# One burst of twelve score tiles for two pairs of heads, in the attention of rounds two to four of a float32 attention and gated-MLP kernel

## The chip, the cores and the metric

The kernel runs on one core of a Trainium2 chip. The metric is device time in microseconds (us). Before the change it is 634.46 us, the median of three runs (633.99 to 634.55).

## The reference, cut to what matters

```python
scores = scale * np.matmul(q, k.transpose(0, 1, 3, 2)) - np.log(S)   # scale = 1/8
attn = 1.0 / (1.0 + np.exp(-scores))                                  # a sigmoid, no softmax
x = np.matmul(attn, v)            # 8 batches, 12 heads, S = 448, 64 wide; then [8, 448, 768]
h = np.maximum(x @ w_in, 0.0)     # w_in [768, 1024]
u, v = h[..., :512], h[..., 512:]
v_n = (v - mean(v)) / np.sqrt(var(v) + 1e-06)
v_s = np.einsum('ts,bsd->btd', w_spatial, v_n) + b_spatial[None, :, None]
return ((u * v_s) @ w_out).astype(np.float32)
```

All in float32. The change touches only the first three lines' part of the program.

## The kernel before, in words

**Rounds.** Two batches make a round, so there are four (`m` = 0 to 3, called rounds one to four here). A round does the attention of its two batches, then the MLP (`v_half`, `spatial`, `u_half`, `outputs`). Round one has an attention of its own (`first_attention`); `attention(m)` (L1107) does rounds two to four. It is a generator: `outputs` of the round before runs its first two pieces (`splits(0)` and `splits(1)`) at its two `between()` calls, L982 and L994, and the main loop the rest (L1345).

**Units and pairs.** A unit is one load of two heads' q and k (tile `raw`, four buffers). Two neighbouring units share one load of v (tile `v`, three buffers) and make a pair; a round has six pairs, p = 0 to 5, units 2p and 2p + 1. A unit's q and k are cut into a high float32r part and a rest (`attention_splits`, L291, into a tile `qks` of three buffers): a copy (L116) and a subtraction (L117), which stand on VectorE except for the first units of a round.

**A pair** (`pair`, L1164). Six score tiles: for each, `attention_scores` (L309) issues three matmul steps for two heads side by side (64 rows each, L339) into a PSUM tile of two banks, and ScalarE applies the sigmoid (L347) from there to an SBUF tile `at`. Then the splits for the next pair are issued (L1177). Then six product tiles (`attention_values`, L353): `at` times v, two heads side by side (64 columns each, float32, L373), added up in one more PSUM tile, `pav`. `copy_sums` (L1148, with the copy in L1150) has VectorE copy `pav` to a tile `whole`. TensorE's records show a product matmul as two.

**PSUM.** `banks` (L128) hands out four tiles in turn, the one longest not handed out first. Scores and `pav` alike take them: seven a pair.

**SBUF.** Ten tags (`big`, `tmp`) hold the `at` tiles and the `whole` tiles, handed out from the list `free`. Every finished pair keeps one for its `whole`.

**The rest of keys.** 448 keys are three tiles of 128 and a rest of 64. The rests of all pairs are done after pair 4 in two groups of three, p = 0, 3, 1 and then 4, 2, 5 (`short_scores`, L1138, and `short_values`): their operands come by loads of their own, tile `last`, two DMAs each (`last_loads`, L1125; 64 KB and 448 KB). Pair 5 comes after them.

**Order of queues.** Each engine's instructions run in the order in which they are emitted (`in_program_order`, L19). So does SyncE (SP), which issues all these DMAs and waits where a buffer isn't free yet. After pair p the loop at L1200 issues the next loads of q and k (L1203) or `last` (L1206), a load of v (L1212), which waits until pair p's products have read the buffer, some weight work (`load_weights`; in round two this is GpSimd's `u_sums` and `v_sums`, with stores to HBM), and in rounds three and four a load of factors (`block_load`, L1195).

Of the kernel before, what the change touches and what calls it, by code (L numbers as in the profile page):

```python
# [9 lines left out]
F32 = mybir.dt.float32  # L10
F32R = mybir.dt.float32r
U32 = mybir.dt.uint32
AF = mybir.ActivationFunctionType
ALU = mybir.AluOpType

P = 128
# [20 lines left out]
def attn_gmlp_kernel(  # L37
# [25 lines left out]
    nc = tc.nc  # L63
    B, NHP, _, _ = qk.shape
    S = out.shape[3]
    D = P // 2
    NCC = out.shape[1]
    DM = NCC * P
    F = w_in.shape[1] // (4 * NCC)
# [9 lines left out]
    QK = 1.0 / math.sqrt(D)  # L79
# [43 lines left out]
    def slot(tags, name, shape=(P, 2, 512), dtype=F32):  # L123
        tag = tags.pop(0)
        tags.append(tag)
        return work.tile(list(shape), dtype, tag=tag, name=name, bufs=1)
# [134 lines left out]
    def load_weights(n):  # L261
        for _ in range(n):
            next(weights[0], None)
# [24 lines left out]

    parts_of = {}

    def attention_splits(b, hp):  # L291
        raw = loaded[b, hp][:, HALF:]
        s = work.tile([P, 2, 2 * S], F32R, tag="split", name=f"qks_{b}_{hp}", bufs=3)
        if b == 0 and hp < 2:

            for cols, copy in ((slice(REST, PART), nc.vector.tensor_copy), (slice(0, FULL - P), nc.scalar.copy)):
                split(s[:, 0, cols], s[:, 1, cols], raw[:, cols], nc.vector.tensor_copy if hp else copy)
        else:
            scalar = b == 1 or b == 0 and hp not in (1, 2) or b % 2 == 0 and b and hp < 2
            split(s[:, 0, :PART], s[:, 1, :PART], raw[:, :PART], nc.scalar.copy if scalar else nc.vector.tensor_copy)  # L300
        parts_of[b, hp] = s
# [7 lines left out]
    def attention_scores(b, hp, t, tag=None, slots=big, raws=None):  # L309

        psc = banks(f"psc_{b}_{hp}_{t}", tag)
        heads = [slice(j * D, (j + 1) * D) for j in range(2)]
        if t == NFULL:
            for odd in range(2):
                if raws is None:
                    raw = loaded[b, hp + odd]
                    key, query = raw[:, :HALF], raw[:, HALF + REST :]
                else:
                    key, query = raws[:, odd, :HALF], raws[:, odd, HALF:]
                for j, rows in enumerate(heads):  # L320
                    nc.tensor.matmul(  # L321
                        psc[odd * HALF : (odd + 1) * HALF, j, :S],
                        key[rows],
                        query[rows],
                        start=True,
                        stop=True,
                    )
        elif b == hp == 0 and t % (NFULL + 1) == 0:
            raw = loaded[b, t // (NFULL + 1)][:, HALF:]
            for j, rows in enumerate(heads):  # L330
                nc.tensor.matmul(  # L331
                    psc[:, j, :S], raw[rows, FULL - P : FULL], raw[rows, REST:PART], start=True, stop=True
                )
        else:
            s = parts_of[b, hp + t // (NFULL + 1)]
            k = (t % (NFULL + 1) + NFULL - 1) % NFULL * P
            for i, (a, e) in enumerate(FIRST_TERMS if b == hp == 0 else TERMS):
                for j, rows in enumerate(heads):
                    nc.tensor.matmul(  # L339
                        psc[:, j, :S],  # L340
                        s[rows, a, k : k + P],
                        s[rows, e, REST:PART],
                        start=i == 0,
                        stop=i == len(TERMS) - 1,
                    )
        at = slot(slots, f"at_{b}_{hp}_{t}")[:, :, :S] if isinstance(slots, list) else slots
        nc.scalar.activation(at, psc[:, :, :S], AF.Sigmoid, bias=bias_s, scale=QK)  # L347
        return at
# [4 lines left out]
    def attention_values(b, hp, t, at, last_v=None, tag=None):  # L353

        key = b, hp, last_v is None
        if key not in pav_of:
            pav_of[key] = banks(f"pav_{b}_{hp}_{t}", tag)
        pav = pav_of[key]
        total = NFULL + 1 if b < 2 else NFULL if last_v is None else 1
        for odd in range(2):  # L360
            if t == NFULL:
                rows = slice(odd * HALF, (odd + 1) * HALF)
            elif (t > NFULL) == odd:
                rows = slice(0, P)
            else:
                continue
            unit = key, odd
            count[unit] = count.get(unit, 0) + 1
            start, stop = count[unit] == 1, count[unit] == total
            vt = values[b, hp][:, t] if last_v is None else last_v  # L370
            for j in range(2):
                heads = slice(j * D, (j + 1) * D)
                nc.tensor.matmul(pav[heads, odd, :S], vt[rows, heads], at[rows, j], start=start, stop=stop)  # L373
        return pav[:, :, :S]

    def x_parts(b, hp):
# [206 lines left out]

    xs = {}

    others = [const.tile([P, 2, F // 2], F32R, name=f"other_{i}") for i in range(2)]
    other_places = [t.rearrange("p a f -> p (a f)")[:, 16 : 16 + S] for t in others]

    v_second, x_rest = {}, {}

# [516 lines left out]
    def attention(m):  # L1107

        first = 2 * NHP * m
        free = []  # L1110
        shorts, wholes, lasts, held = {}, {}, {}, {}
        copy = nc.vector.tensor_copy

        def unit(p):
            return units[first + 2 * p]

        def loads(*ns):
            for n in ns:
                attention_loads(*units[first + n])

        def splits(*ns):
            for n in ns:
                attention_splits(*units[first + n])

        def last_loads(p):  # L1125
            b, hp = unit(p)
# [21 lines left out]
        def copy_sums(p, pav, copy):  # L1148
            whole = slot(free, f"whole_{m}_{p}")[:, :, :S]
            copy(whole, pav)  # L1150
            wholes[p] = free.pop(), whole
# [12 lines left out]
        def pair(p):  # L1164
            full, tags = [], []
            for t in (*FIRST, *SECOND):
                if p == NHP - 1 and t == TILES - 1:
                    place = work.tile([P, 2, S], F32, tag="v", name=f"at_last_{m}", bufs=3)
                    full.append((*unit(p), t, attention_scores(*unit(p), t, None, place)))
                else:  # L1170
                    full.append((*unit(p), t, attention_scores(*unit(p), t, None, free)))
                    tags.append(free.pop())
            if p < 2:
                load_weights(1)
            nc.scalar.copy(mark, full[-1][-1][:1, 0, :1])
            if p + 1 < NHP:
                splits(2 * p + 2, 2 * p + 3)  # L1177
            for args in full:
                pav = attention_values(*args)
            free.extend(tags)  # L1180
            if p + 1 < NHP:
                copy_sums(p, pav, copy)
            return pav

        splits(0)
        yield
        splits(1)
        yield
        free.extend((*big, *tmp))
        if m == 1:  # L1190
# [4 lines left out]
        def block_load(k):  # L1195
            nc.sync.dma_start(v_block(m, k).bitcast(F32), w_v_dram[:, k])

        loads(4, 5)
        value_loads(*unit(2))
        for p in range(NHP - 1):  # L1200
            pair(p)
            if p < 3:
                loads(2 * p + 6, 2 * p + 7)  # L1203
            else:
                for u in ((0, 3), (1, 4, 2, 5))[p - 3]:
                    last_loads(u)  # L1206
            if p == 2:
                last_v = work.tile([P, 2 * NFULL + 1, P], F32, tag="v", name=f"last_v_{m}", bufs=3)
                lasts_of = v[2 * m : 2 * m + 2, :, :, NFULL].rearrange("b g p c -> p b g c")
                for i, b, gs in ((0, 0, slice(0, 2)), (2, 0, slice(2, 3)), (3, 1, slice(0, 3))):  # L1210
                    nc.sync.dma_start(last_v[:, i : i + gs.stop - gs.start], lasts_of[:, b, gs])
            elif p < 4:  # L1212
                value_loads(*unit(p + 3 - p // 3))
            load_weights((1, 1, 2, 3, 8)[p])
            if m > 1 and p < 4:
                block_load(p)
            elif m == 1 and p == 4:
                for k in range(4):
                    block_load(k)
        first_ones, others_of = (0, 3, 1), (4, 2, 5)  # L1220
        for p in first_ones:
            short_scores(p)
# [44 lines left out]
        xs.update({(S2, c): unit_of(raws[c]) for c in range(NH)})  # L1267
        xs[S1, 0] = unit_of(raws[3])
        xs[S4, 0], xs[S3, 0], xs[S1, 1], xs[S4, 1], xs[S4, 2], xs[S3, 2] = free
        xs[S1, 2] = tuple(other_places)  # L1270
        xs[S3, 1] = tuple(part[:, :S] for part in parts)
        for c in range(NH):
            xs[A11, c], xs[A12, c] = (halves(x_s[:, :, 2 * c + i, :S]) for i in range(2))
# [161 lines left out]
```

## Time and profile before

| | |
|---|---|
| median of three runs | 634.46 us |
| the profiled execution | 635.16 us |
| its span, first to last instruction | 633.4 us |
| TensorE busy | 99% |
| VectorE, ScalarE, GpSimd busy | 70%, 54%, 17% |
| granted TensorE clock, mean | 1.000 |
| score matmuls (L339), product matmuls (L373) | 93.5 and 116.9 us busy |

Busy time of TensorE adds what pipelined matmuls overlap, so it says that the engine is never without work, not how fast it goes. How fast it goes is read from the number of matmuls that start in a stretch. A row of the timeline merges instructions of one kind that follow each other; its time goes from the first start to the last end. In a DMA row the time is that of the issue; the transfer lands later.

### The profile page before, as it was taken

How to read it: one execution, taken by the hardware profiler on the slowest of the kernel's cores; microseconds unless marked ns; L12 is line 12 of the kernel's file. 1: busy time of each engine (PE TensorE's matmuls, PEld its weight loads, DVE VectorE, ACT ScalarE, POOL GpSimd, SP SyncE). 2: the span in 40 equal slices, each digit the busy share in tenths (PEclk: the TensorE clock that was granted, in tenths of full speed). 3: DMA queues.
4: the chain of work that ended last, by engine and by line, in shares of the span. 5: the costliest groups of instructions: out<-in, count | busy, mean ns of one | idle time of the engine just before them, and what ended most of it. 6: DMA issues, size and time to landing. Idle time of an engine off the chain costs nothing.

```text
span 633.4 us, 10382 instructions
## 1 busy us (share of the span) xinstructions
PE 629.1 (99%) x4029; PEld 492.5 (78%) x4029; DVE 440.3 (70%) x649; ACT 343.0 (54%) x548; POOL 108.5 (17%) x168
## 2 busy tenths in 40 slices
PE   9999999999999999999999999999999999999997
PEld 5545789999855479999975549999996545999997
DVE  6888779998866697456764489635775549845485
ACT  5888385215366776712346687660317668673040
POOL 0000111064969741100000003110000001210000
PEclk9999999999999999999999999999999999999999
DMA  8776741156797776362277824508028681451303
GB/s 313 256 283 196 253 133 33 35 199 254 267 349 244 250 273 227 116 219 107 76 272 252 287 73 153 203 38 324 25 109 308 238 274 51 160 190 51 100 29 146
DMA packets 47746, 116.66 MB, mean 184 GB/s; under 512 B 9040, under 2 KB 26320, under 8 KB 47440
## 3 DMA queue, kind: packets, MB, share of 16 engines
q1 hardware_dynamic: 47696, 115.98, 52.6%
q8 instruction: 32, 0.52, 0.3%
q14 instruction: 18, 0.15, 0.1%
HBM read 91.59 MB, written 24.38 MB: 183 GB/s over the span
## 4 chain that ended last, share of the span: by engine, by line
PE 99%; DVE 0%; issue 0%
PE pav L373 21%; PE pv L392 17%; PE psc L339 14%; PE pw L392 11%; PE pg L392 11%; PE ux L392 7%; PE uy L392 5%; PE pu L392 5%; PE px L392 4%; PE psc L321 3%; PE idle L1332 0%; PE psc L331 0%; PE last L392 0%; DVE cs L1004 0%
## 5 line engine op out<-in xcount | busy, mean ns | idle before, releaser
L347 ACT ACTIVATE at<-psc,bias_s 128x896 f32<-128x896 f32 x165 | 152.9, 1015 | 95.3 <-PE psc L339 78.5
L373 PE MATMUL pav<-at,v 128*64 128x448 f32 (+1 forms) x612 | 116.9, 543 | 0.0
L339 PEld LDWEIGHTS psc<-qks 64*128 64x128 f32 x852 | 78.7, 186 | 21.6 <-issue 14.3
L339 PE MATMUL psc<-qks 64*128 64x448 f32 x852 | 93.5, 369 | 0.0
L373 PEld LDWEIGHTS pav<-at,v 128*64 128x64 f32 (+1 forms) x612 | 40.0, 136 | 64.7 <-issue 45.0
L392 PE MATMUL pg<-w_sp_s,vn 128*128 128x448 f32 x352 | 71.7, 362 | 0.0
L392 PEld LDWEIGHTS pg<-w_sp_s,vn 128*128 128x128 f32 x352 | 65.8, 187 | 4.4
L412 POOL CAST tail<-x_s 128x128 fp32r<-128x128 f32 x40 | 19.3, 517 | 274.3 <-ACT x_s L1158 199.0
L117 DVE TENSOR_TENSOR qks<-raw,qks 128x848 fp32r<-128x848 f32 (+2 forms) x50 | 53.5, 1078 | 5.6 <-ACT qks L116 4.4
L1150 DVE COPY whole<-pav 128x896 f32<-128x896 f32 x15 | 16.4, 1092 | 57.3 <-PE pav L373 57.3
L392 PE MATMUL pw<-x_s,factors 128*128 128x448 f32 x261 | 54.1, 362 | 0.0
L392 PEld LDWEIGHTS pw<-x_s,factors 128*128 128x128 f32 x261 | 48.9, 187 | 3.6 <-DVE x_s L887 0.3
L479 DVE SCALAR_TENSOR_TENSOR vn<-rv,rstd,vn 128x512 fp32r<-128x512 f32 (+1 forms) x26 | 18.8, 748 | 23.6 <-ACT vn L472 23.5
L392 PE MATMUL ux<-x_s,w_u_s 128*128 128x448 f32 x162 | 33.4, 362 | 0.0
L392 PEld LDWEIGHTS ux<-x_s,w_u_s 128*128 128x128 f32 x162 | 30.4, 188 | 2.0
L392 PEld LDWEIGHTS pv<-factors,x_s 128*128 128x128 f32 x243 | 28.0, 188 | 2.1 <-issue 2.1
L392 PE MATMUL pu<-x_s,w_u_s 128*128 128x448 f32 x144 | 29.1, 362 | 0.0
L392 PE MATMUL pv<-factors,x_s 128*128 128x256 f32 x243 | 28.9, 278 | 0.0
L392 PEld LDWEIGHTS pu<-x_s,w_u_s 128*128 128x128 f32 x144 | 27.0, 187 | 1.8
L472 ACT ACTIVATE vn<-rv,rstd 128x512 fp32r<-128x512 f32 (+1 forms) x26 | 17.9, 720 | 18.3 <-POOL rstd L461 18.2
L460 POOL TENSOR_SCALAR rstd<-power 128x1 f32<-128x1 f32 (+1 forms) x19 | 4.5, 237 | 130.3 <-ACT pv L458 95.2
L864 ACT CAST x_s<-g 128x896 fp32r<-128x896 f32 x6 | 5.7, 942 | 38.5 <-DVE g L863 38.5
(198 smaller groups left out, 1060.4 us busy)
## 6 DMA issues: line engine op xcount, KB each, us to landing
raw<-qk_dram SPq DMA_DIRECT2D x46, 456.0 KB, 6.1
v<-v_dram SPq DMA_DIRECT2D x23, 448.0 KB, 5.7
factors<-w_v_dram SPq DMA_DIRECT2D x12, 768.0 KB, 5.8
factors<-t_dram SPq DMA_DIRECT2D x12, 768.0 KB, 4.6
last<-qk_dram SPq DMA_DIRECT2D x18, 448.0 KB, 5.2
factors<-tv_dram SPq DMA_DIRECT2D x9, 768.0 KB, 5.8
factors<-tu_dram SPq DMA_DIRECT2D x9, 768.0 KB, 4.3
wraw<-w_in_dram SPq DMA_DIRECT2D x12, 512.0 KB, 5.9
```

The costliest lines, as they stand in the source:

```text
L117: nc.vector.tensor_sub(lo, src, hi.bitcast(F32))
L321: nc.tensor.matmul(psc[odd * HALF : (odd + 1) * HALF, j, :S], key[rows], query[rows], start=True, stop=True,)
L339: nc.tensor.matmul(psc[:, j, :S], s[rows, a, k : k + P], s[rows, e, REST:PART], start=i == 0, stop=i == len(TERMS) - 1,)
L347: nc.scalar.activation(at, psc[:, :, :S], AF.Sigmoid, bias=bias_s, scale=QK)
L373: nc.tensor.matmul(pav[heads, odd, :S], vt[rows, heads], at[rows, j], start=start, stop=stop)
L392: nc.tensor.matmul(ps, st, mv, start=start and i == 0, stop=i == len(ops) - 1, skip_group_check=not start)
L412: nc.gpsimd.tensor_copy(tails[hp // 2][a][:, :, part], x.bitcast(F32))
L460: nc.gpsimd.tensor_scalar(rstd[:, :n], power[:, :n], 1.0 / F, 1e-6, op0=ALU.mult, op1=ALU.add)
L472: nc.scalar.mul(hi, rvs[i][rows], rstd[rows, i : i + 1])
L479: nc.vector.scalar_tensor_tensor(lo, rvs[i][rows], rstd[rows, i : i + 1], hi.bitcast(F32), op0=ALU.mult, op1=ALU.subtract,)
L864: copy(both[:, 0], b)
L1150: copy(whole, pav)
```

## The change

In rounds two to four two pairs are done together by a new function, `double`: all twelve score tiles come first, then all twelve product tiles. In round two these are pairs 1 and 2; in rounds three and four pairs 1 and 2 and pairs 3 and 4. The other pairs stay as they were.

Of the twelve score tiles, 2, 4 and 6 are copied from PSUM to their `at` tile by VectorE, and ScalarE applies the sigmoid to them later, in place. Products start with tile 0; tiles 9, 10 and 11 take the `at` tiles of 0, 1 and 3 once these are used up. In pairs 3 and 4 there are only seven tags, and two more `at` tiles are made of four tiles of half a size that lie idle then (`other` and `wval`); a tile there is a list of two halves with a sigmoid each.

A double pair needs four units split ahead of it, so `following(p)` issues four splits (or two) in one go. The tile `qks` has three buffers; the fourth unit (5, and 9 in rounds three and four) is split into a part of `x_s`. Loads move with it: those of units 4 and 5 ahead of the last stores of the round before, those of 8 and 9 ahead of the first double pair. What the loop did after a pair is now `after(p)`; for the first pair of a double pair it is called between the products of the two (`between`).

```diff
-    def attention_splits(b, hp):
+    def attention_splits(b, hp, s=None):
         raw = loaded[b, hp][:, HALF:]
-        s = work.tile([P, 2, 2 * S], F32R, tag="split", name=f"qks_{b}_{hp}", bufs=3)
+        if s is None:
+            s = work.tile([P, 2, 2 * S], F32R, tag="split", name=f"qks_{b}_{hp}", bufs=3)
...
+        if slots is None:
+            return psc[:, :, :S]
         at = slot(slots, f"at_{b}_{hp}_{t}")[:, :, :S] if isinstance(slots, list) else slots
...
+        last_of_four = (5,) if m == 1 else (5, 9)
...
-                attention_splits(*units[first + n])
+                attention_splits(*units[first + n], x_s[:, :, NCC - 1] if n in last_of_four else None)
...
-            if p + 1 < NHP:
-                splits(2 * p + 2, 2 * p + 3)
+            splits(*following(p))
             for args in full:
                 pav = attention_values(*args)
...
+        groups = ((0,), (1, 2), (3,), (4,)) if m == 1 else ((0,), (1, 2), (3, 4))
+
+        def following(p):
+            ends = [g[-1] for g in groups]
+            if p not in ends:
+                return ()
+            g = (*groups, (NHP - 1,), ())[ends.index(p) + 1] if p < NHP - 1 else ()
+            return [2 * r + odd for r in g for odd in range(2)]
+
+        def double(p, extra, between):
+
+            tiles = [(*unit(r), t) for r in (p, p + 1) for t in (*FIRST, *SECOND)]
+            ats, tag_of, scores = {}, {}, {}
+            extra_of = {0: 0, 1: 1, 9: 0, 10: 1}
...
+            def sigmoid(k, src=None):
+                src = scores[k] if src is None else src
+                parts = [(a, src[:, j]) for j, a in enumerate(ats[k])] if isinstance(ats[k], list) else [(ats[k], src)]
+                for to, part in parts:
+                    nc.scalar.activation(to, part, AF.Sigmoid, bias=bias_s, scale=QK)
...
+            for k in range(9):
+                score(k)
+                take(k)
+                if k in (2, 4, 6):
+                    copy(ats[k], scores[k])
+                else:
+                    sigmoid(k)
+            for k in (2, 4):
+                sigmoid(k, ats[k])
+            for k in range(9, 12):
+                score(k)
+            ahead_of = following(p + 1)
+            splits(*ahead_of[:2])
+            for k, then in ((0, 9), (1, 10), (3, 11)):
+                product_of(k)
+                take(then)
+                sigmoid(then)
+            product_of(5)
+            sigmoid(6, ats[6])
+            nc.scalar.copy(mark, ats[6][:1, 0, :1])
+            product_of(2)
+            copy_sums(p, product_of(4), copy)
+            between()
+            splits(*ahead_of[2:])
+            for k in range(7, 12):
+                product_of(k)
+            copy_sums(p + 1, product_of(6), copy)
...
         yield
         splits(1)
+        loads(4, 5)
         yield
...
-        loads(4, 5)
         value_loads(*unit(2))
-        for p in range(NHP - 1):
-            pair(p)
-            if p < 3:
-                loads(2 * p + 6, 2 * p + 7)
-            else:
+        last_vs = []
+
+        def after(p):
+            if p == 0:
+                loads(6, 7)
+            elif p == 2:
+                loads(10, 11)
+            elif p > 2:
                 for u in ((0, 3), (1, 4, 2, 5))[p - 3]:
                     last_loads(u)
...
+        extra = []
+        if m > 1:
+            halves_of = [other_tiles(f"oat_{m}", F32)]
+            halves_of.append([work.tile([P, 512], F32, tag="wval", name=f"wat_{m}_{i}", bufs=2) for i in range(2)])
+            extra = [[t[:, :S] for t in ts] for ts in halves_of]
+        for group in groups:
+            if len(group) == 1:
+                pair(*group)
+            else:
+                if group[0] == 1:
+                    loads(8, 9)
+                    load_weights(1)
+                double(group[0], extra if group[0] > 1 else [], lambda: after(group[0]))
+            after(group[-1])
```

## Rows read from the trace of the kernel before

**Rows 1.** The page: busy time of engines, granted clock in 40 slices.

```profile
PE 629.1 (99%) x4029; PEld 492.5 (78%) x4029; DVE 440.3 (70%) x649; ACT 343.0 (54%) x548; POOL 108.5 (17%) x168
...
PEclk9999999999999999999999999999999999999999
```

**Rows 2.** TensorE's timeline, rounds two and three: start, us, what, count.

```profile
167.37 3.88 PE L339 MATMUL psc<-qks 64*128 64x448 f32 x36
...
175.87 3.88 PE L339 MATMUL psc<-qks 64*128 64x448 f32 x36
...
184.33 0.88 PE L339 MATMUL psc<-qks 64*128 64x448 f32 x6
...
363.82 2.49 PE L321 MATMUL psc<-last 64*64 64x448 f32 x24
```

**Rows 3.** Busy time by windows: two inside scores, two inside products.

```profile
176.30:177.30 1.00, 1.00 (x14) 0.94 (x12) 0.78 (x1) 0.51 (x1) 0.92 (x2) 1.00 1.03 400
176.30:179.30 3.00, 3.00 (x34) 2.80 (x32) 2.35 (x3) 2.51 (x3) 2.44 (x4) 1.00 1.03 404
179.90:181.78 1.88, 1.88 (x12) 0.71 (x10) 1.45 (x2) 1.88 (x3) 0.98 (x2) 1.00 1.03 411
179.90:183.66 3.76, 3.76 (x22) 1.43 (x20) 1.45 (x2) 2.58 (x4) 1.66 (x2) 1.00 0.91 361
```

**Rows 4.** ScalarE: sigmoids of a pair; two lines' min/median/max ns.

```profile
176.79 5.50 ACT L347 ACTIVATE at<-psc,bias_s 128x896 f32<-128x896 f32 x6 [2.71 <-PE psc L339]
...
L812 ACT COPY uu<-ux x2: 533/534/534, 264.2 to 266.0; 128x448 f32<-128x448 f32 x2
...
L1158 ACT CAST x_s<-whole x2: 943/944/945, 368.3 to 372.3; 128x896 fp32r<-128x896 f32 x2
```

**Rows 5.** Timeline of VectorE in round two, and one row of GpSimd's.

```profile
164.41 1.34 DVE L117 TENSOR_TENSOR qks<-raw,qks 128x848 fp32r<-128x848 f32 x1
...
170.85 1.68 DVE L116 CAST qks<-raw 128x848 fp32r<-128x848 f32 x1
172.56 1.45 DVE L117 TENSOR_TENSOR qks<-raw,qks 128x848 fp32r<-128x848 f32 x1
175.99 1.09 DVE L1150 COPY whole<-pav 128x896 f32<-128x896 f32 x1 [1.97 <-PE pav L373]
...
173.20 2.21 POOL L622 TENSOR_TENSOR wsum<-wsum,wsum 128x256 f32<-128x256 f32 x2
```

**Rows 6.** Groups of VectorE's splits, 167:200 us, then 321:364 us.

```profile
L117 DVE TENSOR_TENSOR qks<-raw,qks 128x848 fp32r<-128x848 f32 x8 | 11.1, 1392 | 0.3
L116 DVE CAST qks<-raw 128x848 fp32r<-128x848 f32 x8 | 7.6, 951 | 0.6 <-DMA raw<-qk_dram 0.6
...
L117 DVE TENSOR_TENSOR qks<-raw,qks 128x848 fp32r<-128x848 f32 x10 | 10.4, 1042 | 0.3
L116 DVE CAST qks<-raw 128x848 fp32r<-128x848 f32 x10 | 5.9, 594 | 0.0
```

**Rows 7.** Loads of q and k, 160 to 200 us: issue to landing.

```profile
DMA to landing us min/median/max: 4.1/7.3/9.2
```

**Rows 8.** Timeline of SyncE's issues in round three.

```profile
355.46 0.34 SPq L284 DMA_DIRECT2D v<-v_dram  x1
355.85 1.15 SPq L1196 DMA_DIRECT2D factors<-w_v_dram  x1
358.25 4.72 SPq L1136 DMA_DIRECT2D last<-qk_dram  x8
```

**Rows 9.** Landing of the factor loads (355.85, round four's) and `last` (358.25).

```profile
DMA to landing us min/median/max: 6.2/6.2/6.2
...
DMA to landing us min/median/max: 4.7/4.9/6.5
...
L1136 SPq DMA_DIRECT2D last<-qk_dram x2: 378/424/470, 358.2 to 358.7; - x2
DMA to landing us min/median/max: 4.1/4.9/5.7
```

More of the change, by code (lines that the diff above doesn't have):

```diff
@@ L372, in attention_values @@
                 heads = slice(j * D, (j + 1) * D)
-                nc.tensor.matmul(pav[heads, odd, :S], vt[rows, heads], at[rows, j], start=start, stop=stop)
+                nc.tensor.matmul(pav[heads, odd, :S], vt[rows, heads], at[j][rows] if isinstance(at, list) else at[rows, j], start=start, stop=stop)
         return pav[:, :, :S]
@@ L584, in attn_gmlp_kernel, with other_tiles @@
     xs = {}
-    others = [const.tile([P, 2, F // 2], F32R, name=f"other_{i}") for i in range(2)]
-    other_places = [t.rearrange("p a f -> p (a f)")[:, 16 : 16 + S] for t in others]
+    def other_tiles(name, dtype=F32R):
+        return [const.tile([P, F], dtype, tag=f"other_{i}", name=f"{name}_{i}") for i in range(2)]
+    late_others = other_tiles("other")
+    others = [t.rearrange("p (a f) -> p a f", a=2) for t in late_others]
     v_second, x_rest = {}, {}
@@ L1183, in pair, with score, take, product_of @@
             return pav
+        groups = ((0,), (1, 2), (3,), (4,)) if m == 1 else ((0,), (1, 2), (3, 4))
[9 more added lines that the diff above has]
+            extra_of = {0: 0, 1: 1, 9: 0, 10: 1}
+            def score(k):
+                scores[k] = attention_scores(*tiles[k], None, None)
+            def take(k):
+                if extra and k in extra_of:
+                    ats[k] = extra[extra_of[k]]
+                else:
+                    b, hp, t = tiles[k]
+                    ats[k] = slot(free, f"at_{b}_{hp}_{t}")[:, :, :S]
+                    tag_of[k] = free.pop()
+            def sigmoid(k, src=None):
[3 more added lines that the diff above has]
+                    nc.scalar.activation(to, part, AF.Sigmoid, bias=bias_s, scale=QK)
+            def product_of(k):
+                pav = attention_values(*tiles[k], ats[k])
+                if k in tag_of:
+                    free.append(tag_of.pop(k))
+                return pav
+            for k in range(9):
[25 more added lines that the diff above has]
+            copy_sums(p + 1, product_of(6), copy)
@@ L1208, in attention @@
                 last_v = work.tile([P, 2 * NFULL + 1, P], F32, tag="v", name=f"last_v_{m}", bufs=3)
+                last_vs.append(last_v)
                 lasts_of = v[2 * m : 2 * m + 2, :, :, NFULL].rearrange("b g p c -> p b g c")
@@ L1219, in attention @@
                     block_load(k)
+        extra = []
[6 more added lines that the diff above has]
+                pair(*group)
+            else:
+                if group[0] == 1:
[3 more added lines that the diff above has]
+            after(group[-1])
+        last_v, = last_vs
         first_ones, others_of = (0, 3, 1), (4, 2, 5)
@@ L1269, in attention @@
         xs[S4, 0], xs[S3, 0], xs[S1, 1], xs[S4, 1], xs[S4, 2], xs[S3, 2] = free
-        xs[S1, 2] = tuple(other_places)
+        xs[S1, 2] = tuple(t[:, 16 : 16 + S] for t in (other_tiles(f"xo_{m}") if m > 1 else late_others))
         xs[S3, 1] = tuple(part[:, :S] for part in parts)
```

## The prediction

> **What bounds the kernel now.** I read the page's busy shares and clock first [rows 1]: TensorE is busy 99% of the span, its granted clock is in the top tenth in all 40 slices, and no other engine is above 78%. So a change gains only where it shortens TensorE's own stream, and loses wherever TensorE has to wait; there is no idle time to take away. The order of time on TensorE then shows what the stream of a round is made of [rows 2]: six score tiles, six product tiles, and so on. From one burst of scores to the next is 184.33 - 175.87 = 8.46 us (8.50 for the pair ahead of it, from 167.37; I use 8.47). Inside a burst, windows opened in its middle give the steady rate [rows 3]: 34 - 14 = 20 score matmuls in 2.00 us, so two in 0.200; 22 - 12 = 10 product matmuls in 1.88 us, so two in 0.376. (A window also counts what was under way when it opened; the difference takes that out.) A pair of 36 scores and 24 product matmuls would take 18 x 0.200 + 12 x 0.376 = 8.11 us at these rates. The other 0.36 us is spent at the two borders, from scores to products and back.
>
> **The change part by part.** *Borders.* A burst of twelve followed by twelve products has one border each way where two pairs had two: 0.36 us less. There are five such double pairs (one in round two, two each in rounds three and four): 5 x 0.36 = 1.8 us gained. This is the whole gain; the matmuls stay the same in number and shape. If part of the 0.36 is not paid at the border but once in each tile, it is less; zero is the lower end.
>
> *Emptying PSUM.* There are four PSUM tiles, so score tile k waits for tile k-4 to be emptied. Sigmoids go at 5.50 / 6 = 0.92 us each [rows 4] against 0.60 for three matmul steps of a tile, so ScalarE alone would hold up twelve. With tiles 2, 4 and 6 copied by VectorE at 1.09 us (the copy of sums has the same shape and source [rows 5]) I lay the burst out from its start: tile k can be read at 0.92 + 0.60 k; the sigmoids of 0, 1, 3, 5, 7, 8 end by 1.9, 2.9, 3.8, 4.9, 6.1, 7.1, the copies at 3.2, 4.4, 5.6. Tile 5 needs the second sigmoid at 3.1 (as before the change), tiles 6, 8, 10 the copies at 3.7, 4.9, 6.1, the first product's PSUM tile the sigmoid of 8 at 7.4. Each is met by 0.2 us or more: nothing added. The three sigmoids on SBUF and tiles 9 to 11 then lie beside the products: six times 0.92 from 7.1 on end by 12.7, with tile 9 due at 13.5 and 6 at 15.7. No row shows a sigmoid that reads SBUF; the nearest, a cast of the same size from SBUF, is 0.94 [rows 4], and even 1.3 each would be in time. In the second double pair of a round four tiles are split into halves; a 128x448 copy is 0.53 [rows 4], 1.07 for two against 1.01 for one. On the two that lie ahead of tile 5 that costs 0 to 0.1; I take 0.
>
> *The splits ahead of the first double pair.* Here the change costs something. The first pair of a round now issues four splits on VectorE, not two, and its copy of sums stands behind all four, as VectorE works in order. The fourth score tile of the double pair takes that copy's PSUM tile (seven tiles are taken in a pair, from four). In round two it is due 1.91 us after the burst starts: 175.87 + 1.91 = 177.78. Before the change the second split ends at 172.56 + 1.45 = 174.0 [rows 5]. The two added ones cost there (window 167 to 200) 1.392 + 0.951 = 2.34 us each, in round three 1.042 + 0.594 = 1.64 [rows 6]: in round two GpSimd is at work on weights [rows 5]. So 174.0 + 2 x 2.34 = 178.7, the copy 1.09, ready at 179.8: **TensorE waits 2.0 us** (1.9 with the 0.1 by which operations on VectorE overlap). With 1.64 it is 0.6; at the price of the split from 170.85 to 174.0, 3.15, it is 3.6. The Trainium skill, SBUF — State Buffer, section "SBUF: two separate sides", says the pair of ports that VectorE and GpSimd share is an exclusive lock whose loser blocks for the whole instruction. By it each of a split's two operations could lose a whole GpSimd operation, the price would be nearer the 3.15 and the time 1.7 us above my sum; the trace agrees that a split costs more beside GpSimd, 2.34 against 1.64, and its mean says that it loses less often than each time. The loads of those two units are moved ahead of the last stores. They would issue near 165.8 (the second split of the round ends there [rows 5]) and land 4.1 to 9.2 later [rows 7], 170 to 175, so mostly in time; what they are moved past, three stores, isn't waited for by TensorE. In rounds three and four no GpSimd work stands beside: two splits more, each 1.6, start when the first pair's scores are read (its start + 3.9) and end by 7.2, with the copy due at 8.6: no cost.
>
> *SyncE's queue at the end of rounds three and four.* SyncE issues in order too. The load of the last pair's values waits for the fourth pair's (p = 3) products, at 355.46 in round three; then come a factor load and, behind them, the short score operands (`last`) from 358.25 on [rows 8]. The third of these to be used is the first that comes behind that wait. Before, the short scores start at 363.82 [rows 2], 8.36 us after the wait ended. The double pair lasts 2 x 8.47 - 0.36 = 16.6 us, and the short scores start then. Its wait ends with six product tiles still to come, 12 x 0.376 = 4.5 us, so near 12.2 with a tenth for the last product's end: 4.4 us ahead of the short scores instead of 8.36. The third short tile is due after four of the burst's six steps, 1.56: at **18.1**. The queue: value load 12.2, factor load 12.55, whose issue takes 0.4 to 1.15, the third operand's small part at 13.0 to 13.75 and its large one 0.42 behind, 13.4 to 14.2. The large one lands 5.7 us after its issue behind that factor load [rows 9], and nothing says it would be faster when it follows more closely: 13.9 + 5.7 = 19.6. **TensorE waits 1.5 us in each of two rounds: 3.0.** If it lands in the 4.1 of the small one the wait is 0; if the factor load takes 6.5 and the operand lands 2.3 behind it, as at 358.7 + 5.7 against 355.85 + 6.2, it is 21.3 and the wait 3.2. The later operands follow while the first products run; they are due 4.7 us after the first. The loads for units 8 and 9, put ahead of the double pair, have some 12 us to land.
>
> *Sum.* -1.8 + 1.9 + 3.0 = +3.1 us. Against the profiled execution (635.16 us, span 633.4 and 1.76 around it) that is 638.3; the median shown, 634.46, is 0.70 below that execution, so the forecast is 634.46 + 3.1 = **637.6 us**.
>
> **The rivals.** *Neither wait decides.* If splits in round two cost 1.64 and the third operand lands within 4.2 us, the borders are left: 634.46 - 1.8 + 0.6 = 633.3, or 632.7 with no wait at all. For it: SyncE's landings do vary, 4.7 to 6.5 for one factor load [rows 9]; against it: both waits would have to vanish, and GpSimd's work is there. This is the other side: it decides where the third short operand has landed by 18.1 and the copy of sums is done by 177.8. *Only the splits decide.* The operand lands in time, the splits cost their 1.9: 634.46 + 0.1 = 634.6, no change. *The clock falls.* A wait of 2 to 3 us could let the granted clock go from 2.4 to 1.2 GHz for a stretch; no row shows it fall, since TensorE never waits here. [...] *The burst is not a burst.* If VectorE's copies come 0.4 us late in each double pair 2.0 of the gain is lost and the waits stay: 639.6.
>
> **How the numbers follow.** A difference under about 0.2%, 1.3 us, can't be told from none here. Forecast with both waits at some size: 0.53. Only the splits (or waits that just eat the gain): 0.17, no change. Neither: 0.25, faster. Late burst 0.03, clock 0.02, both slower. So slower 0.58, same 0.17, faster 0.25. Forecast's own range, each wait taken half-way to its ends: splits 1.25 to 2.75, operands 1.5 to 4.7 for the two rounds, so 634.46 - 1.8 + 2.75 = 635.4 to 634.46 - 1.8 + 7.45 = 640.1. The range with the others reaches down to 632.6, the full gain, and up to 640.1; what it leaves out is the late clock, both waits at their upper ends and part of the fastest cases.
>
> **What would show it.** Right: 72 scores in one stretch of 7.4 us with no gap, five double pairs of 16.6 us; in round two a gap of about 2 us at the fourth score tile, released by VectorE's copy of sums; in rounds three and four a gap near 1.5 us within the first short scores, released by the operand's load; clock unchanged. Wrong: no gap at either place (then the gain is bare), gaps inside the bursts released by VectorE's copies or ScalarE, or a double pair that isn't shorter than two pairs.

## The result, and the profile after

The changed kernel takes 639.25 us, the median of six runs (637.08 to 642.18), against 634.23 us before: a ratio of 1.0079, 95% interval 1.0052 to 1.0105, so slower by 5.0 us. Measured again beside the experiments, on another occasion, it took 637.6 us against 634.49, a ratio of 1.0049 (1.0036 to 1.0061), 3.1 us. Its runs lie 5 us apart; those of the kernel before lie within 1 us on the first occasion and 1.7 on the second. Where the difference comes from is a result of its own, told below.

The page shows what [rows 1] showed: TensorE busy throughout, the clock in the top tenth in every slice of this execution (637.67 us, span 635.9 against 633.4).

```profile
PE 627.0 (99%) x4029; PEld 493.3 (78%) x4029; DVE 456.2 (72%) x664; ACT 344.5 (54%) x551; POOL 107.2 (17%) x168
...
PEclk9999999999999999999999999999999999999999
```

What the page hides stands in the waits of TensorE: who waited, for whom, us in total, times, the longest. The kernel before had one such row only, 0.8 us ahead of its first matmul; the changed kernel has that one and these three:

```profile
PE psc L322 <- DMA last<-qk_dram: 2.3, 3, 1.1
PE psc L340 <- DVE whole L1157: 2.0, 1, 2.0
...
PE psc L332 <- DMA raw<-qk_dram: 0.6, 1, 0.6
```

The first two rows are the waits that the prediction named, with a small one of round two beside them. The third lies 6.6 us into round one, ahead of all that the change moves; the same kernel in e1 has it at 0.3, and e2 to e9 don't have it. TensorE's timeline of round two (start, us, what, count, the idle time ahead and its releaser) shows the wait for VectorE's copy, and answers to [rows 2]:

```profile
166.96 3.89 PE L340 MATMUL psc<-qks 64*128 64x448 f32 x36
...
175.46 2.08 PE L340 MATMUL psc<-qks 64*128 64x448 f32 x18
179.56 3.88 PE L340 MATMUL psc<-qks 64*128 64x448 f32 x36 [2.02 <-DVE whole L1157]
183.28 1.97 PE L340 MATMUL psc<-x_s 64*128 64x448 f32 x18
185.18 9.24 PE L376 MATMUL pav<-at,v 128*64 128x448 f32 x48
...
217.87 0.98 PE L322 MATMUL psc<-last 64*64 64x448 f32 x8 [0.18 <-DMA last<-qk_dram]
```

The burst of twelve score tiles breaks off after 18 matmuls, that is three tiles. The fourth begins 2.02 us after TensorE ran dry, released by L1157, VectorE's copy of sums. (The step from one matmul pair to the next is 2.39 us there where 0.20 is usual, so 2.19 us are lost; a row's idle time is a little less, as it counts from a matmul's end. Over the burst it is 2.3: from its start to the first product are 185.18 - 175.46 = 9.72 us, where e9 below, with no wait, has 7.42.) The last row is a small wait of the same round, for short operands. VectorE's timeline tells why the copy is late, to be read against [rows 5]:

```profile
167.60 1.03 DVE L116 CAST qks<-raw 128x848 fp32r<-128x848 f32 x1
...
170.61 1.67 DVE L116 CAST qks<-raw 128x848 fp32r<-128x848 f32 x1
172.31 1.45 DVE L117 TENSOR_TENSOR qks<-raw,qks 128x848 fp32r<-128x848 f32 x1
173.69 1.12 DVE L116 CAST qks<-raw 128x848 fp32r<-128x848 f32 x1
174.85 1.46 DVE L117 TENSOR_TENSOR qks<-raw,qks 128x848 fp32r<-128x848 f32 x1
176.22 1.13 DVE L116 CAST x_s<-raw 128x848 fp32r<-128x848 f32 x1
177.39 1.12 DVE L117 TENSOR_TENSOR x_s<-raw,x_s 128x848 fp32r<-128x848 f32 x1
178.43 1.08 DVE L1157 COPY whole<-pav 128x896 f32<-128x896 f32 x1
```

The two added splits follow each other without a pause, 2.5 and 2.2 us from start to start (the two ahead of them, from 167.60 and 170.61, took 3.0 and 3.1), and the copy of sums starts at 178.43 although pair 0's products had ended near 175.5. The operand loads had landed in time: nothing in these rows waits for one.

Round three, TensorE again:

```profile
331.69 5.68 PE L340 MATMUL psc<-qks 64*128 64x448 f32 x54
...
348.27 5.85 PE L340 MATMUL psc<-qks 64*128 64x448 f32 x54
...
365.03 1.73 PE L322 MATMUL psc<-last 64*64 64x448 f32 x16
367.79 0.98 PE L322 MATMUL psc<-last 64*64 64x448 f32 x8 [1.03 <-DMA last<-qk_dram]
```

Here the first double pair is whole: 348.27 - 331.69 = 16.58 us, against 2 x 8.47 = 16.94. The second, to 365.03, takes 16.76. Then the short scores stop after two of three tiles for 1.03 us. SyncE's issues and the landing of the third tile's two loads answer to [rows 8, 9]:

```profile
360.63 0.34 SPq L284 DMA_DIRECT2D v<-v_dram  x1
361.01 0.43 SPq L1269 DMA_DIRECT2D factors<-w_v_dram  x1
361.55 5.00 SPq L1143 DMA_DIRECT2D last<-qk_dram  x8
```

```profile
L1143 SPq DMA_DIRECT2D last<-qk_dram x2: 379/424/468, 361.5 to 362.0; - x2
...
  PE psc L322: 1.0, 1
...
DMA to landing us min/median/max: 4.9/5.3/5.7
```

The value load waits until 360.63 for the fourth pair's products, and the operands stand behind it: the large one goes out near 361.97, lands 5.7 us later at 367.7, and the matmuls start at 367.79.

### The profile page after: what moved, and what is told of

Same layout as the page of the kernel before. It is cut to its first block, busy times and chain, and to the rows that moved or that the text cites. A ratio compares the mean times of both kernels' runs of the same rounds, so it can differ in the third digit from the quotient of the medians.

```text
span 635.9 us, 10415 instructions
## 1 busy us (share of the span) xinstructions
PE 627.0 (99%) x4029; PEld 493.3 (78%) x4029; DVE 456.2 (72%) x664; ACT 344.5 (54%) x551; POOL 107.2 (17%) x168
## 4 chain that ended last, share of the span: by engine, by line
PE 77%; DVE 13%; DMA 5%; issue 2%; SPq 1%; ACT 1%; POOL 0%; DVEq 0%
PE pav L376 16%; PE pv L395 12%; PE psc L340 12%; PE pw L395 11%; PE pg L395 8%; PE ux L395 7%; PE uy L395 5%; PE px L395 3%; DMA last<-qk_dram 3%; PE psc L322 2%; DVE wval L149 1%; DVE wval L152 1%; DVE qks L116 1%; DVE vn L482 1%; DMA v_vals_dram<-wval 1%
## 5 line engine op out<-in xcount | busy, mean ns | idle before, releaser
L350 ACT ACTIVATE at<-psc,bias_s 128x896 f32<-128x896 f32 x105 | 98.2, 1014 | 73.3 <-PE psc L340 53.1
L376 PE MATMUL pav<-at,v 128*64 128x448 f32 (+1 forms) x580 | 110.0, 542 | 0.0
L376 PEld LDWEIGHTS pav<-at,v 128*64 128x64 f32 (+1 forms) x580 | 38.4, 136 | 62.0 <-issue 48.2
L340 PEld LDWEIGHTS psc<-qks 64*128 64x128 f32 x762 | 69.6, 184 | 20.1 <-issue 10.8
L340 PE MATMUL psc<-qks 64*128 64x448 f32 x762 | 82.7, 366 | 2.0 <-DVE whole L1157 2.0
L117 DVE TENSOR_TENSOR qks<-raw,qks 128x848 fp32r<-128x848 f32 (+2 forms) x45 | 47.1, 1057 | 5.4 <-ACT qks L116 4.4
L1157 DVE COPY whole<-pav 128x896 f32<-128x896 f32 x15 | 16.4, 1091 | 36.6 <-PE pav L376 36.6
L1221 ACT ACTIVATE at<-psc,bias_s 128x896 f32<-128x896 f32 x37 | 35.6, 1010 | 12.1 <-PE psc L340 11.9
```

The source lines that it names most:

```text
L117: nc.vector.tensor_sub(lo, src, hi.bitcast(F32))
L340: nc.tensor.matmul(psc[:, j, :S], s[rows, a, k : k + P], s[rows, e, REST:PART], start=i == 0, stop=i == len(TERMS) - 1,)
L376: nc.tensor.matmul(pav[heads, odd, :S], vt[rows, heads], at[j][rows] if isinstance(at, list) else at[rows, j], start=start, stop=stop)
L1221: nc.scalar.activation(to, part, AF.Sigmoid, bias=bias_s, scale=QK)
```

## The experiments

I compare the kernels by their rounds: from the first score of pair 0 to the first score of pair 5, read from TensorE's timeline of each. This leaves out what lies ahead of round two and behind round four. The stretches between these rounds, and from the last of them to the last twelve matmuls, agree within 0.03 us in all ten profiles. The two ends do not: the first score of round two starts at 167.37 before the change and between 166.31 and 167.29 in the others, and from the start of the last twelve matmuls to the span's end are 5.04 us before and 4.55 to 4.64 in the others.

| kernel (profiled execution) | round two, us | round three | round four | mean clock |
|---|---|---|---|---|
| before | 51.92 | 51.89 | 51.90 | 1.000 |
| the change | 54.07 | 52.44 | 52.55 | 1.000 |
| e1, the change again | 53.95 | 52.70 | 52.75 | 1.000 |
| e2, operand loads first | 56.18 | 51.35 | 51.35 | 0.997 |
| e3, copy of sums earlier | 52.99 | 52.69 | 53.03 | 0.999 |
| e4, both | 53.02 | 51.59 | 51.60 | 1.000 |
| e5, double pair in round two alone | 55.50 | 51.89 | 51.89 | 0.997 |
| e6, single pairs in round two | 51.92 | 52.53 | 52.64 | 1.000 |
| e7, that with operand loads first | 51.92 | 51.35 | 51.34 | 0.999 |
| e8, that with halves later | 51.92 | 51.17 | 51.17 | 1.000 |

**e1: the changed kernel again.** No edit.

> The changed kernel once more, for the spread of its times. Its first profile has two waits of my theory: 2.0 us at the fourth score tile of round two, and 1.0 and 1.1 us at the third short tile of rounds three and four, which with some smaller terms make its span 2.5 us longer; but its median is 5.0 us above the kernel before and its runs lie 5 us apart. Theory: the same waits in another execution, and what differs from run to run is the size of waits for transfers or for GpSimd's weight work in round two (the matmuls' own rates agree to 0.1 us). Expected: median 637 to 641, spread 3 us or more, TensorE's waits in the profile add up to the span's excess over 632 within 1 us. Rival: the matmuls themselves go slower in some executions (a lower granted clock, slower reading of weights); then the waits stay at 4 us and stretches without waits are longer.

Measured: 637.6 us (636.81 to 638.92, five runs) against 634.49. The profile has the same waits, 2.1 us in round two and 1.3 in each of the others. Of its five executions the four with a mean granted clock of 1.000 took 636.81 to 637.75 us, the one at 0.997 took 638.92. In the six of the first occasion two were at 1.000 (637.08 and 637.67), three at 0.997 (638.97 to 639.63) and one at 0.995 (642.18). So most of the spread goes with the clock, the rival, and not with waits of changing size; how long the waits were in executions without a trace is not shown. The spread in this set is 2.1 us, under the 3 expected. The two rows of waits add up to 4.7 us, 1.1 more than the span's excess over 632, so this part of the expectation was missed too, by a little; the shorter end of the span (4.61 against 5.04) is a part of it.

**e2: the operand loads first.** In rounds three and four the loads for pairs 1 and 4 are issued with those for 0 and 3.

```diff
-                for u in ((0, 3), (1, 4, 2, 5))[p - 3]:
+                for u in (((0, 3), (1, 4, 2, 5)) if m == 1 else ((0, 3, 1, 4), (2, 5)))[p - 3]:
                     last_loads(u)
```

> In rounds three and four the loads of the short scores of pairs 1 and 4 are issued ahead of the value load of the last pair, not behind it. Theory (SyncE's order): the waits of 1.0 and 1.1 us at the third short tile go, the wait of round two stays; about 2.3 us less than the changed kernel run beside it. Rival (these transfers themselves are late, whatever the order, as the DMA engines are full): the waits stay at 0.5 us or more each, under 1 us gained.

Measured: 636.78 us, only 0.8 below e1 by the medians. By rounds the theory holds: rounds three and four take 51.35 us, 0.54 less than before the change, and the waits for the operands are gone there. What hides it is the clock: eight of its ten executions had a mean of 0.997 (636.56 to 637.86 us); the two at 1.000 took 634.24 and 634.52, 3 us less than e1's at 1.000. Its profile is one of the eight and shows where the clock falls. The windows give, in turn, the busy time of TensorE, its weight loads, VectorE, ScalarE and GpSimd, then the granted clock, the DMA share and GB/s:

```profile
174.00:178.00 4.00, 3.24 (x26) 1.83 (x22) 3.93 (x4) 1.90 (x2) 3.70 (x5) 1.00 0.98 399
178.00:180.00 2.00, 0.63 (x4) 0.59 (x6) 2.00 (x3) 0.00 (x0) 1.92 (x4) 0.84 1.04 422
180.00:182.00 2.00, 2.00 (x14) 1.77 (x12) 0.31 (x1) 1.01 (x1) 1.13 (x3) 0.50 1.00 339
182.00:184.00 2.00, 2.00 (x18) 1.82 (x18) 1.35 (x2) 0.94 (x1) 0.03 (x1) 0.80 0.94 281
184.00:186.00 2.00, 2.00 (x24) 1.87 (x22) 1.97 (x3) 1.80 (x3) 1.92 (x3) 1.00 0.77 304
```

TensorE runs dry behind 177 us, for 2.1 us; the granted clock, 1.00 until 178, is 0.84 in the mean of the next 2 us, 0.50 from 180 to 182, that is 1.2 GHz, 0.80 in the mean of the two after that, and 1.00 again. In the timeline the burst that follows the wait stretches:

```profile
175.16 2.08 PE L340 MATMUL psc<-qks 64*128 64x448 f32 x18
179.37 5.46 PE L340 MATMUL psc<-qks 64*128 64x448 f32 x36 [2.13 <-DVE whole L1157]
...
186.56 3.97 PE L376 MATMUL pav<-at,v 128*64 128x448 f32 x19
```

From 175.16 to the first product at 186.56 are 11.40 us, where the change's own profile has 185.18 - 175.46 = 9.72 with a wait shorter by 0.1: the fall of the clock costs 1.6 us. The wait alone does not bring the fall about: e1's profile has a wait of 2.12 us at this place, and its clock is at 1.00 there and in all the 2 us around it, from 174 to 188:

```profile
180.00:182.00 2.00, 2.00 (x24) 1.87 (x22) 1.29 (x2) 1.81 (x2) 1.06 (x2) 1.00 1.08 332
```

**e3: the copy of sums earlier.** The fourth split is issued behind the copy of sums.

```diff
-            splits(*following(p))
+            splits(*following(p)[:3])
             for args in full:
                 pav = attention_values(*args)
             free.extend(tags)
             if p + 1 < NHP:
                 copy_sums(p, pav, copy)
+            splits(*following(p)[3:])
             return pav
```

> In the first pair of a round the fourth split is issued behind the copy of sums, not ahead of it. Theory (VectorE's order): the wait of 2.0 us at the fourth score tile of round two goes, or falls under 0.3, about 2.2 us less than the changed kernel run beside it. Rival (VectorE is simply full in that stretch, by GpSimd's work beside it): the wait moves to tile 9, whose split is now later, and less than 1 us is gained.

Measured: 637.64 us (636.44 to 640.04), no gain on e1 by the median. Neither side had it whole. The wait for the copy of sums is gone and round two gains 1.0 us on e1, but a wait of 0.9 has come in its place, and not at tile 9:

```profile
PE psc L322 <- DMA last<-qk_dram: 2.4, 2, 1.4
PE psc L340 <- DVE at L1234: 0.9, 1, 0.9
```

L1234 is the copy of scores from PSUM. VectorE's timeline of e4, which has the same edit, shows its order there:

```profile
176.68 1.08 DVE L1157 COPY whole<-pav 128x896 f32<-128x896 f32 x1
177.69 0.59 DVE L116 CAST x_s<-raw 128x848 fp32r<-128x848 f32 x1
178.31 1.47 DVE L117 TENSOR_TENSOR x_s<-raw,x_s 128x848 fp32r<-128x848 f32 x1
179.70 3.21 DVE L1234 COPY at<-psc 128x896 f32<-128x896 f32 x3
```

The fourth split, from 177.69, now stands ahead of the three copies, which start at 179.70 and follow each other without a pause. Tile 2 could have been read near 177.9 (its burst begins at 175.80, by the 0.92 + 0.60 k of the prediction). The same order costs rounds three and four 0.25 each, as their rows in the table show for e4 against e2: 51.59 against 51.35.

**e4: both edits.**

> Both edits. Theory: only the borders are left, five times 0.36 less 0.2 for each of the two double pairs with halved sigmoids, 1.4 us: 632.8 to 633.3, faster than the kernel before by 0.2%. If the spread of the changed kernel comes from these two places the runs lie within 1 us of each other; if it comes from elsewhere (the transfers of round two behind GpSimd's work) they still lie 2 us or more apart and the median is above 634.

Measured: 634.33 us against 634.49, a ratio of 1.0002 (0.9993 to 1.0011): no difference. The expectation missed the wait that e3 moved, with smaller ones beside it 1.5 us in round two (53.02 against 51.92 - 0.36), and the 0.25 in each of the others. The runs did draw together: ten of eleven between 633.75 and 635.17.

**e5: the double pair in round two alone.**

```diff
-        last_of_four = (5,) if m == 1 else (5, 9)
+        last_of_four = () if m > 1 else (5,) if m == 1 else (5, 9)
...
+        if m > 1:
+            groups = tuple((r,) for r in range(NHP - 1))
...
+            elif p == 1 and (1,) in groups:
+                loads(8, 9)
```

> Only round two has its double pair; rounds three and four do single pairs as before. Theory: one border saved, 0.36, against the wait for the copy of sums, 2.3 counted from the usual distance of two score matmuls: +1.9 us where the granted clock stays up, and 1.6 us more, +3.5, in executions where it falls to 1.2 GHz behind that wait, as in the profile of the kernel with the operand loads first. So executions of two kinds, told apart by their mean clock. Rival (the clock's fall is a matter of the chip at that moment, not of this wait): executions with a lower mean clock are as rare as in the kernel before, 1 of 22.

Measured: 637.5 us against 634.58, 1.0046 (1.0033 to 1.0058). All five executions had a mean clock of 0.997, so there was one kind and not two. Round two is 3.58 us longer than before the change, the 3.5 expected; the median is only 2.9 longer, as the two ends of the profiled execution are 0.8 shorter. In the kernel before, beside it, all 18 executions were at 0.999 or 1.000. So the fall comes with this wait, of 2.00 us here, and the windows show it right behind:

```profile
180.00:182.00 2.00, 2.00 (x16) 1.79 (x14) 0.72 (x2) 1.01 (x1) 1.39 (x3) 0.56 1.03 386
182.00:184.00 2.00, 2.00 (x16) 1.81 (x14) 0.94 (x1) 1.01 (x1) 0.00 (x0) 0.59 0.95 253
```

**e6: single pairs in round two.** The edit of e5, with `m == 1` in place of `m > 1`.

> Round two does single pairs; rounds three and four are as in the changed kernel. Theory: four borders of 0.36 less the 0.17 that halved sigmoids cost in each of two double pairs, -1.1, and two waits for the short operands of 1.2 each: +1.3 us. As these waits are half as long as that of round two, the clock should fall seldom. Rival (the waits of these rounds come from what round two left late): they go, -1.1 us.

Measured: 635.79 us, 1.0019 (1.0010 to 1.0028), +1.2 us. The waits of 1.2 us each are there, so they do not come from round two, and none of ten executions fell below 0.999.

**e7: that, with the operand loads first** (the edit of e2).

> The same with the loads of the short operands of pairs 1 and 4 ahead of the last value load. Theory: no wait of the change is left: -1.1 us against the kernel before, clock never below 0.999, no gap over 0.1 us in TensorE's stream of rounds two to four. Rival (a border is worth less than the 0.36 worked out from steady rates): under -0.6.

Measured: 632.98 us, 0.9975 (0.9965 to 0.9986), -1.6 us; by rounds -0.54 and -0.56, the -1.1 expected. TensorE's waits in its profile are those of the first microsecond alone.

**e8: that, with the halved tiles later.** In the change's profile ScalarE takes 1.05 us from one halved tile to the next, where a whole one takes 0.92:

```profile
349.19 1.16 ACT L1221 ACTIVATE oat<-psc,bias_s 128x448 f32<-128x448 f32 x2 [4.77 <-PE psc L340]
350.24 1.16 ACT L1221 ACTIVATE wat<-psc,bias_s 128x448 f32<-128x448 f32 x2
```

```diff
-            extra_of = {0: 0, 1: 1, 9: 0, 10: 1}
+            extra_of = {7: 0, 8: 1}
```

> The same, and in the second double pair of a round the halved tiles are 7 and 8, not 0, 1, 9 and 10. Theory: the scores of that double pair take 7.41 instead of 7.59 us, 0.17 us less in each of two, -1.4 us against the kernel before. Rival (the halved sigmoid of 8 now comes too late for the first product's PSUM tile): 0.1 to 0.2 us appear at the start of the products and nothing is gained.

Measured: **632.42 us against 634.58**, a ratio of 0.9966 (0.9954 to 0.9979), -2.2 us, faster than both kernels. By rounds it is -0.72 and -0.73. What the median has beyond these 1.45 us is within the interval, and no experiment tells it apart from the runs' spread; in the profiles it lies at the two ends of the span (round two starts 0.2 us earlier, the end is 0.5 shorter). Both double pairs of round three now have one length:

```profile
329.71 5.67 PE L340 MATMUL psc<-qks 64*128 64x448 f32 x54
...
346.29 5.68 PE L340 MATMUL psc<-qks 64*128 64x448 f32 x54
...
362.88 2.49 PE L322 MATMUL psc<-last 64*64 64x448 f32 x24
```

346.29 - 329.71 = 16.58 and 362.88 - 346.29 = 16.59, and the short scores run through: 24 matmuls in 2.49 us, as in [rows 2].

**e9: GpSimd kept quiet.** e5 with GpSimd's weight work of round two put off until after the double pair.

```diff
+    hush, owed = [False], [0]
...
     def load_weights(n):
+        if hush[0]:
+            owed[0] += n
+            return
         for _ in range(n):
             next(weights[0], None)
...
         splits(0)
+        hush[0] = m == 1
         yield
...
+            if p == 2:
+                hush[0] = False
+                load_weights(owed[0])
+                owed[0] = 0
             load_weights((1, 1, 2, 3, 8)[p])
```

> Only round two has its double pair, and GpSimd's weight work that would run beside the splits ahead of it is put off until the double pair is over (the later weight work then comes late, which may make TensorE wait further on; the verdict lies in the stretch from 165 to 186 us). Theory (VectorE is late because each split costs 2.3 to 2.8 us beside GpSimd's work, against 1.6 without): the four splits take 1.6 each, the copy of sums is done where pair 0's products end, and the wait at the fourth score tile goes from 2.0 us to under 0.7, with the clock staying up. Rival (the splits are late by their count and by when the loads land, not by GpSimd): the wait stays above 1.5 us.

Measured, in one execution: the stretch from 166 to 188 us has no GpSimd work at all. VectorE's splits there:

```profile
170.17 0.60 DVE L116 CAST qks<-raw 128x848 fp32r<-128x848 f32 x1
170.81 1.04 DVE L117 TENSOR_TENSOR qks<-raw,qks 128x848 fp32r<-128x848 f32 x1
171.76 0.60 DVE L116 CAST x_s<-raw 128x848 fp32r<-128x848 f32 x1
...
174.86 1.09 DVE L1162 COPY whole<-pav 128x896 f32<-128x896 f32 x1 [1.42 <-PE pav L381]
```

From 170.17 to 171.76 a split takes 1.59 us where the change had 2.5 and 2.2, the copy of sums starts at 174.86, right behind the products, and the burst is whole:

```profile
174.74 5.68 PE L345 MATMUL psc<-qks 64*128 64x448 f32 x54
180.26 1.97 PE L345 MATMUL psc<-x_s 64*128 64x448 f32 x18
182.16 9.24 PE L381 MATMUL pav<-at,v 128*64 128x448 f32 x48
```

From 174.74 to 182.16 are 7.42 us for 72 scores. Putting the work off also takes its stores out of SyncE's queue, so that loads can go out earlier; that does not explain the quicker splits, since those of the change follow each other with no wait for a load. The work put off is paid for later and dearly, as the loads for the short operands stand behind its stores on SyncE, and the whole takes 655.31 us:

```profile
PE psc L327 <- DMA last<-qk_dram: 18.0, 3, 13.2
```

## Why the prediction was right, point by point

**The bound.** Right: in the rounds every wait of TensorE came out in the time. The rounds of the change's profile are 2.15, 0.55 and 0.65 us longer, 3.35 in all, against +3.1 forecast. The terms below make this up: -1.44 for borders, 2.3 for the splits, 1.1 and 1.2 for SyncE's order, and 0.2 for the small wait of round two. The span is only 2.5 longer, as its two ends are 0.8 shorter, which I didn't have. The executions at full clock (636.81 to 637.75) lie around the 637.6 forecast. That the sum came so near is in part luck: borders and splits came out 0.4 worse each, the operands 0.7 better. That the first median, 639.25, lies in the range is luck too: the range's upper end stands for longer waits, and by the mean clocks what took the time there was the clock.

**Borders: 1.8 forecast, 1.44 in the change, 0.36 for each double pair without halves.** 0.36 is a border's price as worked out from the steady rates: e8's four double pairs give it four times. In the change two of five lost 0.17 to 0.18 by the halved sigmoids, which I took at 0 of "0 to 0.1". That range was too low, and e8 takes the loss away by moving the halves. The row chosen was a copy (0.53); two halved sigmoids take 1.16 from the first start to the last end, and the time from tile to tile is 1.05.

**Emptying PSUM.** Right: in rounds three and four the first double pair has no gap, and the copies by VectorE are in time. In e3 and e4 VectorE has a split ahead of them and they are not, so the margin was as thin as laid out.

**The splits: 1.9 forecast, 2.2 measured at the tile, 2.3 over the burst.** Mechanism and place as predicted, a little dearer. The two added splits took 2.4 us in the mean, near the 2.34 of the sum; the copy ended at 178.43 + 1.08 = 179.5, 4.05 us after the burst's start, where I had 3.8. e9 shows the cause by taking it away: without GpSimd beside it no wait is left, not even the 0.6 of the lower end. There two splits of 1.64 were put behind the 174.0 of the profile before; in e9 all four were quick, so the first two ended earlier, too. The Trainium skill, SBUF — State Buffer, "SBUF: two separate sides", has an exclusive lock on a pair of ports that the two engines share. The trace agrees that a split takes longer beside GpSimd, by 0.6 to 0.9 us in the two added (2.2 and 2.5 against e9's 1.59) and by some 1.4 in the two ahead of them; which operation stood behind which is not read from it.

**SyncE's order: 1.5 a round forecast, 1.1 and 1.2 measured.** e2 and e7 take it away by the order alone. The term was a little large for two reasons. The factor load took 0.43 us to issue, not the 1.15 of [rows 8], so the operand went out at 361.97, 13.7 after the double pair's start and not 13.9; it landed after the 5.7 us of [rows 9]. And the halved sigmoids made the double pair 16.76 long and not 16.6, so the third short tile was due later by 0.2. Small ones of the same kind stand in round two, 0.18 in the change and up to 0.6 in e2, where loads stand behind the stores of GpSimd's work. I had none there.

**The clock.** I gave its fall 0.02 and treated it as another case; it is a part of the likeliest one, in some executions. A mean clock of 0.997 or less came in four of six, one of five, eight of ten and five of five executions (the change twice, e2, e5). The two of them that left a trace, of e2 and e5, show the fall behind the wait of round two; for the others the place is inferred. So on the first occasion the median was 639.25 and not 637.6. I had reasoned that no row showed it fall, which was true because no row showed TensorE waiting. For its price I had no row either; by the traces one fall costs 1.6 us, behind one of the three waits and not behind each.

Open: why the clock falls behind one such wait and not behind another of the same length (with five to ten executions of each kernel the shares may differ by chance in part); what else goes with it, as the executions with a lower mean clock are 1.5 to 2.7 us longer than the others of their set, and the one at 0.995 is 4.8 longer; and why the two ends of the span are shorter than in the one profile of the kernel before, which is where the profiles of e7 and e8 have the 0.5 to 0.7 us that their medians have beyond their rounds.

## What to carry to other kernels

On an engine that is never idle, a reordering pays the small steady price of each switch, 0.36 us here, and one late helper behind a queue can cost six times that. For each step that is moved, follow the in-order queues of the helpers: what now stands ahead of the copy that frees a PSUM tile, and which load is now issued behind a wait that used to be over. And look at the granted clock of every execution: a wait of 2 us here cost nearly twice its length in the executions in which the clock fell behind it.

## What the runs showed of the hardware that was not expected

A gap of 2.0 to 2.1 us, in a stream of matmuls that had run for more than 150 us with no wait, took the granted clock from 1.00 to 0.50, 2.4 to 1.2 GHz, in the profiles of e2 (2.13 us) and e5 (2.00). In the profiles of the change (2.02) and e1 (2.12) it did not, so the length of the gap did not decide. By the mean clock it happened in 18 of the 26 executions of these kernels. Ten executions with gaps of 1.1 to 1.2 us (e6) and eleven with one near 1 us (e4) kept mean clocks of 0.999 or 1.000; of five with gaps of 0.9 to 1.4 (e3) one was at 0.997. After the fall the clock was back at 1.00 from 184 us on in both profiles, with TensorE at work without a pause since 179.4 and 179.6.
